# A decode kernel with attention over a long cache and a small MLP: each of the MLP's three tables read in two transfers instead of one

## The chip, the core and the metric

The kernel runs on one core of a Trainium2 chip. The metric is the device time of one execution in microseconds; the time shown for a kernel is the median of its runs. A profile is one further execution, recorded instruction by instruction and packet by packet. Its times count from the first instruction, and its span ends with the last one.

## The reference, cut to what matters

One token `x` of 448 numbers goes through two branches, which a gate mixes:

```
q = x @ wq                                   # 16 heads of 256
p = softmax(q . k_cache / 16)                # 8 K/V heads, 65536 cached positions each
a = (p @ v_cache) @ wo
h = layernorm(x)
u = gelu(h[d] * w1[f] + b1[f])               # 448 x 1792
b = sum over f of u[d, f] * w2[f]  + b2
g = sigmoid(sum(x * gate_w))
out = g * a + (1 - g) * b
```

The cache is 512 MB in bf16 (K and V, 8 heads, 65536 positions, 256 numbers). `wq` and `wo` are 3.5 MB each. The small MLP's `w1`, `b1` and `w2` are 1792 numbers each, 3.5 KB.

## The kernel before, in words

**The stream.** The cache is cut into 32 blocks of 16384 positions. A block of K, and a block of V, is 8 MB, 64 KB on each of 128 partitions. SBUF has one place for a block of V (`vt`) and three half places for K (`k_all`, slots 0 to 2). Blocks of K and V are fetched in turn by SyncE's queue (SP): `load_k_whole` (L132) and `load_v` (L135). For each block VectorE (DVE) transposes K (L402), TensorE (PE) forms the scores (L410), a softmax follows, and PE multiplies the probabilities into V (L430). Blocks 0 to 29 run in a loop of 15 turns with two blocks each (L597); the last two blocks are written out behind it.

**The start.** Before the loop stands work that is done once. SP issues three transfers: the tail of `wq` (`wq_t`, L159, 0.5 MB), the rest of it (`wq_m`, L162, 3 MB), and block 0 of K, called K0 here (L174, which calls L132). V0 is fetched inside the loop, at its first turn. ScalarE (ACT) issues the small transfers from its own queue: `x` (L158), the three tables (L168), the two halves of `gate_w` (L170) and `b2` (L173). Behind them on ACT stand a table load and a square root (L264) for the layer norm, then 14 GELU activations (L280) and the gate's exponential (L340).

**The tables.** Each table is brought in as 14 rows of 128 numbers, 256 bytes a row, and the three stand one below the other in `tables` (42 rows). One PE product with an identity (L255) turns them into columns, in `hd_ps`. DVE copies the columns out (L265, L266), goes on with the layer norm (L267 to L274, then L275, which writes `h_bc`), and ACT applies the GELU of `h_bc` with a column of `w1` as scale and one of `b1` as bias. `w2`'s columns are the weights of 14 PE products (L344).

**The order of work.** `seq` chains the instructions of each engine in the order in which the program is written. On PE the product of the tables (L255) stands ahead of the 128 products that form `q` (L291, L298), and these ahead of the MLP's products (L344). On DVE the copy L265 stands ahead of the rest of the layer norm, of the copies that place `q`, of the gate's sum (L338, L339) and of `mixer_tail` (L349 to L360), which the built program puts before the loop. At the loop's entry all engines meet at a barrier.

**The counters of the transfers.** The framework has eight completion counters for transfers and deals them out in turn. A transfer that is dealt a counter for a second time is not issued until the earlier transfer with that counter has landed; its queue waits there, with everything behind it. Before the loop they are dealt so:

| counter | 0 | 1 | 2 | 3 | 4 | 5 | 6 | 7 | 0 again | 1 again |
|---|---|---|---|---|---|---|---|---|---|---|
| transfer | x | wq_t | w1 | b1 | w2 | wq_m | gate_w a | gate_w b | b2 | K0 |

So `b2` (ACT) waits for `x`, and K0 (SP) for `wq_t`.

Of the kernel before, what the change touches and what calls it, by code (L numbers as in the profile page):

```python
# [33 lines left out]
def kernel(  # L34
# [15 lines left out]
    nc = tc.nc  # L50
# [5 lines left out]
    NF = F // 128  # L56
# [6 lines left out]
    def seq(ins):  # L63
        e = ins.ins.engine
        if e in last:
            tc.add_manual_dep(
                ins.ins,
                last[e],
                mybir.DependencyInfo(
                    mybir.DependencyClass.NoSync, mybir.DependencyReason.DATA  # L70
                ),
                reason="program order",
            )
        last[e] = ins.ins.name
        return ins
# [31 lines left out]
    tables = const.tile([3 * NF, 128], BF16)  # L107
# [43 lines left out]
    def load_v_last(n):  # L151
# [8 lines left out]
        out=wq_t[:, :], in_=A_wq[DM:D, :].rearrange("r (h n) -> (r h) n", h=2)  # L160
    ))
    seq(nc.sync.dma_start(out=wq_m, in_=A_wq[0:DM, :].rearrange("(p k) n -> p k n", k=3)))  # L162
    for k, table in enumerate((
        B_w1[0].rearrange("(b p) -> b p", p=128),
        B_b1.rearrange("(b p) -> b p", p=128),
        B_w2.rearrange("(b p) o -> b (p o)", p=128),
    )):
        seq(nc.scalar.dma_start(out=tables[k * NF:(k + 1) * NF, :], in_=table))  # L168
    for n0, n1 in ((0, D // 2), (D // 2, D)):
        seq(nc.scalar.dma_start(  # L170
            out=gw[:, n0:n1], in_=gate_w.rearrange("(o n) -> o n", o=1)[:, n0:n1]
# [14 lines left out]
        out=val[:], in_=rowsel[:, :, :, 0:NI], op=ALU.add, axis=AXIS.XY  # L186
    ))
    fst = const.tile([128, 2, REP], FP32)
    for e in range(2):
        seq(nc.vector.tensor_reduce(  # L190
            out=fst[:, e, :], in_=rowsel[:, :, :, e:e + 1], op=ALU.add, axis=AXIS.XY
# [3 lines left out]
        out=par[:], in_=ident_f[:].rearrange("p (a r) -> p r a", r=REP), op=ALU.add, axis=AXIS.X  # L195
# [3 lines left out]
        out=nval[:], in0=val[:], scalar1=-scale, scalar2=None, op0=ALU.mult  # L199
# [7 lines left out]
        out=same[:], in_=val[:].unsqueeze(1).to_broadcast([128, 64, REP])  # L207
# [8 lines left out]
        out=sel[:],  # L216
        in_=ident.rearrange("p (w k) -> p w k", w=NW).unsqueeze(2).to_broadcast([128, NW, NQ, 32]),
# [7 lines left out]
        out=xrr[:], in_=xr[:, DM:D].unsqueeze(2).to_broadcast([1, D - DM, 2])  # L225
    ))
    x_col = hd_ps[:, 40:44]
    for k in range(3):
# [13 lines left out]
        out=xtm[:], in0=par[:], scalar1=x_col[:, 3:4], scalar2=None, op0=ALU.mult  # L242
# [19 lines left out]
        out=veps[:], in0=mv[:, 1:2], scalar1=1e-5, scalar2=None, op0=ALU.add  # L262
# [5 lines left out]
    for _ in range(2):  # L268
# [3 lines left out]
            out=ntmp[:], in0=ntmp[:], scalar1=-0.5, scalar2=1.5, op0=ALU.mult, op1=ALU.add  # L272
# [3 lines left out]
        out=h_bc, in0=xf, scalar1=mv[:, 0:1], scalar2=rstd[:, 0:1],  # L276
        op0=ALU.subtract, op1=ALU.mult,
    ))
    for b in range(NF):
        seq(nc.scalar.activation(  # L280
            out=gel[b], in_=h_bc, func=ACT.Gelu_apprx_tanh,
# [33 lines left out]
    for k in range(2):  # L315
        seq(nc.vector.tensor_copy(
            out=qq[:, :, :, k, :], in_=qq_ps.rearrange("p (w g r) -> p w g r", g=HKV, r=REP)
# [314 lines left out]
    for n in (L - 1, L):  # L632
# [9 lines left out]
        else:  # L642
            load_v_last(L)
            for c in range(2):
                seq(nc.sync.dma_start(
                    out=wo_sb[:, 1, c],
                    in_=A_wo.rearrange("(h p c) n -> h p c n", p=128, c=2)[HQ - 1, :, c],
# [3 lines left out]
        else:  # L651
            def rest_base():
# [9 lines left out]
                out=lsv[:], in0=val[:], scalar1=lsum[:, 0:1], scalar2=None, op0=ALU.mult  # L662
# [8 lines left out]
                out=rdv[:], in0=rdv[:], scalar1=gcol[:, 0:1], scalar2=None, op0=ALU.mult  # L671
# [6 lines left out]
    for c in range(2):  # L678
# [9 lines left out]
        out=oT[:], in0=o_last, in1=rdv[:].unsqueeze(1).to_broadcast([128, 2, REP]), op=ALU.mult  # L688
# [43 lines left out]
```

## Time and profile before

| | |
|---|---|
| median of 3 runs | 1263.75 us (1263.6 to 1263.8) |
| span of the profiled execution | 1262.4 us |
| median less span | 1.35 us, which lie outside the first and the last instruction |
| PE busy | 820.4 us (65%) |
| DVE busy | 711.3 us (56%) |
| ACT busy | 75.7 us (6%) |
| read from HBM | 544.22 MB, 431 GB/s over the span |

Queue q1 holds SP's transfers and q10 holds ACT's. A transfer is split into packets on up to 16 rings, one on each DMA engine. On each ring a transfer ends with a packet of 4 bytes that counts it as landed there. The busy share of DMA is the mean over the 16 DMA engines; in a window of a few tenths of a microsecond it can pass 100%, because a packet is counted whole where it starts.

### The profile page before, as it was taken

Reading aid. Unit: us, or ns where it says so; the run is one execution under the profiler, and the core shown is the slowest. Engines: PE = TensorE matmul, PEld = TensorE weight load, DVE = VectorE, ACT = ScalarE, POOL = GpSimd, SP = SyncE. Lnnn points to the kernel's source line nnn. Section 1 sums busy time; section 2 is a strip of 40 time slices with the busy share of each in tenths; the row PEclk is TensorE's granted clock in tenths of the full one; section 3 lists DMA queues with packets and bytes.
Section 4 is the critical chain, followed back from the end, with each engine's and each line's share of the span. In section 5 each row is a group of like instructions: output and inputs, shape, how many; then the busy total and the mean of one; then the engine's idle time right before and its main releaser. Section 6 shows DMA issues by size and latency. Waiting matters only on the chain.

```text
span 1262.4 us, 12359 instructions
## 1 busy us (share of the span) xinstructions
PE 820.4 (65%) x4818; PEld 330.4 (26%) x4818; DVE 711.3 (56%) x755; ACT 75.7 (6%) x163; POOL 4.8 (0%) x9
## 2 busy tenths in 40 slices
PE   4756567575666746676565766648666576665668
PEld 2222122222222312222222322213222232221224
DVE  5665456654556644566544665446654456654575
ACT  4000000000000000000000000000000000000000
POOL 1000000000000000000000000000000000000000
PEclk9987787777887887888778787789777787877888
DMA  9999999999999999999999999999999999999998
GB/s 414 432 437 432 435 432 434 437 432 425 446 432 418 451 416 436 430 437 436 435 432 439 432 432 439 432 439 432 432 439 432 439 432 432 439 432 435 423 432 355
DMA packets 11768, 544.36 MB, mean 431 GB/s; under 512 B 1548, under 2 KB 2062, under 8 KB 2926
## 3 DMA queue, kind: packets, MB, share of 16 engines
q1 hardware_dynamic: 11666, 544.22, 99.7%
q8 instruction: 6, 0.10, 0.0%
q14 instruction: 4, 0.03, 0.0%
q10 hardware_dynamic: 92, 0.01, 0.0%
HBM read 544.22 MB, written 0.00 MB: 431 GB/s over the span
## 4 chain that ended last, share of the span: by engine, by line
DMA 69%; PE 13%; DVE 12%; issue 4%; SPq 0%; ACT 0%; DVEq 0%
DMA k_all<-in_A_k_cache_dram 67%; DVE kT L402 12%; PE sc L410 12%; DMA k_all<-in_A_v_cache_dram 2%; PE pv_last L555 0%; PE hd_ps L546 0%; PE f L555 0%; SPq L153 0%; PE f L693 0%; PE sm_ps L532 0%; ACT p_sb L498 0%; DVE rmax L467 0%; SPq L132 0%; PE hd_ps L532 0%; PE sm_ps L485 0%
## 5 line engine op out<-in xcount | busy, mean ns | idle before, releaser
L410 PE MATMUL sc<-kT,qz 128*128 128x512 bf16 x2048 | 545.7, 416 | 320.1 <-DVE kT L402 319.9
L402 DVE STREAM_TRANSPOSE kT<-k_all 128x2048 f32<-128x2048 f32 x256 | 570.9, 2283 | 208.3 <-DMA k_all<-in_A_k_cache_dram 159.0
L410 PEld LDWEIGHTS <-qz 128*128 128x128 bf16 x2048 | 211.2, 103 | 653.4 <-issue 474.2
L430 PE MATMUL pv_ps<-vt,pT 128*4 128x512 bf16 x1968 | 170.9, 523 | 27.2 <-DVE pT L505 27.2
L511 DVE SCALAR_TENSOR_TENSOR acc<-acc,al,pv_ps 128x512 f32<-128x512 f32 x31 | 23.2, 748 | 159.3 <-PE pv_ps L430 159.3
L430 PEld LDWEIGHTS <-pT 128*4 128x4 bf16 x2000 | 56.6, 108 | 128.9 <-issue 82.7
L498 ACT ACTIVATE p_sb<-sc,nb 128x512 bf16<-128x512 f32 x32 | 22.0, 687 | 1022.6 <-DVE nb L494 1022.6
L467 DVE TENSOR_REDUCE rmax<-sc 128x1 f32<-128x512 f32 x32 | 22.1, 692 | 63.7 <-PE sc L410 63.7
L505 DVE STREAM_TRANSPOSE pT<-p_sb 128x512 bf16<-128x512 bf16 x32 | 22.8, 711 | 27.1 <-ACT p_sb L498 27.1
L517 PE MATMUL hd_ps<-lsum,same 128*128 128x1 f32 x30 | 7.6, 322 | 28.8 <-DVE lsum L506 28.8
L485 PE MATMUL sm_ps<-mrun,ones_f 1*128 1x2 f32 x64 | 12.1, 256 | 21.2 <-DVE mrun L484 13.0
L471 PE MATMUL sm_ps<-ident_f,rmax 128*1 128x128 f32 x32 | 8.6, 270 | 24.5 <-DVE rmax L467 24.5
L555 PE MATMUL pv_last<-wo_in,steps 128*128 128x448 bf16 x64 | 15.6, 368 | 5.4 <-PEq L597 5.4
L555 PEld LDWEIGHTS <-steps 128*128 128x128 bf16 x128 | 11.6, 101 | 22.6 <-issue 14.4
L485 PEld LDWEIGHTS sm_ps<-mrun,ones_f 1*128 1x128 f32 x64 | 9.4, 182 | 27.4 <-DVE mrun L484 16.3
L550 DVE TENSOR_TENSOR a_acc<-a_acc,hd_ps 1x448 f32<-1x448 f32 x15 | 9.1, 608 | 12.9 <-PE hd_ps L546 12.9
L546 PE MATMUL hd_ps<-wo_sb,oT 128*1 128x448 bf16 x60 | 16.4, 365 | 0.0
L559 ACT CAST wo_sb<-pv_last 128x448 bf16<-128x448 f32 x16 | 8.5, 532 | 122.8 <-PE pv_last L555 122.8
L555 PE MATMUL f<-wo_in,steps 128*128 128x448 bf16 x64 | 15.5, 367 | 0.0
L562 ACT COPY wo_sb<-wo_sb 128x896 bf16<-128x896 bf16 x15 | 14.1, 937 | 15.3 <-PE hd_ps L546 15.3
L542 DVE CAST oT<-hd_ps 128x2 bf16<-128x2 f32 x15 | 2.4, 159 | 21.0 <-PE hd_ps L532 21.0
L517 PEld LDWEIGHTS hd_ps<-lsum,same 128*128 128x128 f32 x30 | 6.3, 261 | 30.1 <-DVE lsum L506 30.1
(124 smaller groups left out, 197.2 us busy)
## 6 DMA issues: line engine op xcount, KB each, us to landing
k_all<-in_A_k_cache_dram SPq DMA_DIRECT2D x2, 4096.0 KB, 16.1
vt<-in_A_v_cache_dram SPq DMA_DIRECT2D x1, 5120.0 KB
k_all<-in_A_v_cache_dram SPq DMA_DIRECT2D x1, 4096.0 KB
wo_in<-in_A_wo_dram SPq DMA_DIRECT2D x15, 224.0 KB, 27.9
vt<-in_A_wq_dram SPq DMA_DIRECT2D x1, 3072.0 KB, 10.5
vt<-in_A_v_cache_dram SPq DMA_DIRECT2D x1, 3072.0 KB
k_all<-in_A_v_cache_dram SPq DMA_DIRECT2D x1, 2048.0 KB
k_all<-in_A_v_cache_dram SPq DMA_DIRECT2D x1, 1024.0 KB, 22.6
```

Of the source, the lines that this page charges most:

```text
L402: seq(nc.vector.transpose(out=kT_tiles[i % 2][:].rearrange("p j w k c -> p (j w k c)").bitcast(FP32), in_=slots[pair[i // 4]][:, i % 4 * N ...
L410: seq(nc.tensor.matmul(sc_tiles[e][:, :], lhsT=qz[:, 2 * w + c, 2 * (NI - i):2 * (NI - i) + 128], rhs=kT_tiles[i % 2][:, :, w, :, c], star ...
L430: seq(nc.tensor.matmul(dst[32 * grp:32 * grp + 2 * REP, :, :], lhsT=pT[:, 32 * jj + 2 * REP * ip:32 * jj + 2 * REP * (ip + 1)], rhs=pairs( ...
L467: seq(nc.vector.tensor_reduce(out=rmax[:], in_=sc_ps[:, :], op=ALU.max, axis=AXIS.X))
L485: seq(nc.tensor.matmul(sm_ps[:, 128:128 + REP], lhsT=ones_f[0:1, :], rhs=mrun[0:1, :], start=True, stop=True))
L498: seq(nc.scalar.activation(out=p_sb[:, :], in_=sc_ps[:, :], func=ACT.Exp, scale=scale, bias=nb[:, 0:1], accum_out=den[:, 0:1],))
L505: seq(nc.vector.transpose(out=pT[:, :], in_=p_sb[:, :]))
L511: seq(nc.vector.scalar_tensor_tensor(out=acc[:], in0=acc[:], scalar=al_tiles[e][:, 0:1], in1=src[:, :, :], op0=ALU.mult, op1=ALU.add,))
L517: seq(nc.tensor.matmul(hd_ps[:, 460:461], lhsT=same[:].rearrange("p a r -> p (a r)"), rhs=lsum[:, 0:1], start=True, stop=True,))
L546: seq(nc.tensor.matmul(a_ps, lhsT=oT[:, c, r:r + 1], rhs=wo_sb[:, r, c, :], start=(r == 0 and c == 0), stop=(r == REP - 1 and c == 1),))
L555: seq(nc.tensor.matmul(wo_ps[c], lhsT=steps[:, WS - u:WS - u + 128], rhs=wo_in[:, 2 * u + c, :], start=(u == 0), stop=(u == WS - 1),))
L562: seq(nc.scalar.copy(out=wo_sb[:, 0], in_=wo_sb[:, 1]))
```

## The change

Each table is read in two transfers, cut at a row that differs from table to table: 12 and 2 rows of `w1`, 8 and 6 of `b1`, 4 and 10 of `w2`. The rows land where they did before. ACT issues six transfers where it issued three; the bytes and the rows are the same. Lines behind the edit move down by three.

```diff
-    for k, table in enumerate((
-        B_w1[0].rearrange("(b p) -> b p", p=128),
-        B_b1.rearrange("(b p) -> b p", p=128),
-        B_w2.rearrange("(b p) o -> b (p o)", p=128),
+    for k, (cut, table) in enumerate((
+        (12, B_w1[0].rearrange("(b p) -> b p", p=128)),
+        (8, B_b1.rearrange("(b p) -> b p", p=128)),
+        (4, B_w2.rearrange("(b p) o -> b (p o)", p=128)),
     )):
-        seq(nc.scalar.dma_start(out=tables[k * NF:(k + 1) * NF, :], in_=table))
+        for r0, r1 in ((0, cut), (cut, NF)):
+            seq(nc.scalar.dma_start(
+                out=tables[k * NF + r0:k * NF + r1, :], in_=table[r0:r1, :]
+            ))
```

With three more transfers the counters are dealt differently. `w1a` is the first piece of `w1`, and so on:

| counter | 0 | 1 | 2 | 3 | 4 | 5 | 6 | 7 | 0 | 1 | 2 | 3 | 4 |
|---|---|---|---|---|---|---|---|---|---|---|---|---|---|
| transfer | x | wq_t | w1a | w1b | b1a | wq_m | b1b | w2a | w2b | gate_w a | gate_w b | b2 | K0 |

So now `w2b` waits for `x`, `gate_w a` for `wq_t`, `gate_w b` for `w1a`, `b2` for `w1b`, and K0 on SP's queue waits for `b1a`. The product of the tables (L255 before, L258 after) waits for six transfers instead of three. The order of instructions on PE and DVE is the same.

## The prediction

> **What bounds the kernel now.** I read the page first (slices, chain of waits), then the windows, then the time order of the first 50 us, then the DMA packets in narrow windows.
>
> ```profile
> span 1262.4 us, 12359 instructions
> DMA  9999999999999999999999999999999999999998
> DMA 69%; PE 13%; DVE 12%; issue 4%; SPq 0%; ACT 0%; DVEq 0%
> 60.00:1190.00 1130.00, 731.49 (x4141) 290.89 (x4134) 630.79 (x640) 55.88 (x129) 0.00 (x0) 0.81 1.00 434
> ```
>
> The last row is a window: its last two figures are the DMA share, 1.00, and 434 GB/s. From 60 to 1190 us the 16 DMA engines never rest, while PE and DVE do. So the end is set by the stream of K and V. Whatever fits under it costs nothing. A pause of the stream is never made up, because there is no idle time behind it: it comes out at the end one for one. The change touches the first microseconds, so the question is whether the stream pauses there. The queue that feeds it, in order of time (SPq is SP's issuing):
>
> ```profile
> 0.73 0.42 SPq L159 DMA_DIRECT2D vt<-in_A_wq_dram  x1
> 4.17 0.33 SPq L132 DMA_DIRECT2D k_all<-in_A_k_cache_dram  x1
> 27.06 0.35 SPq L135 DMA_DIRECT2D vt<-in_A_v_cache_dram  x1
> 45.11 0.34 SPq L132 DMA_DIRECT2D k_all<-in_A_k_cache_dram  x1
> ```
>
> These issue `wq_t`, K0, V0 and K1. The stream has a transfer in hand at all times only if each is issued before the one ahead has drained.
>
> ```profile
> q10 hardware_dynamic: 2, 0.00, 1.1%
> ...
> q1 hardware_dynamic: 1, 0.00, 15.0%
> ...
> DMA packets 16, 0.07 MB, mean 177 GB/s; under 512 B 0, under 2 KB 0, under 8 KB 16
> ...
> DMA packets 34, 1.05 MB, mean 2017 GB/s; under 512 B 18, under 2 KB 18, under 8 KB 18
> ...
> DMA packets 31, 0.99 MB, mean 1652 GB/s; under 512 B 15, under 2 KB 15, under 8 KB 15
> ```
>
> These are DMA windows. From 1.5 to 1.78 us q1 has started nothing (only q10 is listed); to 1.80 it has started one packet. So the first packet comes 1.06 us after the issue at 0.73. From 1.78 to 2.15 sixteen start, so the last ring follows within 0.36. From 10.84 to 11.36 there are 18 packets under 512 B: the 16 counts of `wq_m` and two of `gate_w`. There `wq` is over and K0 begins. From 30.2 to 30.8 stand 15 counts: K0 ends, 30.45 in the middle. V0, issued at 27.06, is ready on the rings at 28.1 to 28.5. It has some 2.2 us in hand, and that is all the slack of the start.
>
> **What the tables' transfers cost today.** The q10 packets:
>
> ```profile
> q10 hardware_dynamic: 14, 0.00, 7.9%
> ...
> q10 hardware_dynamic: 84, 0.01, 1.4%
> ...
> DMA packets 29, 0.37 MB, mean 723 GB/s; under 512 B 14, under 2 KB 14, under 8 KB 14
> ...
> q10 hardware_dynamic: 1, 0.00, 2.2%
> q10 hardware_dynamic: 2, 0.00, 5.3%
> q10 hardware_dynamic: 1, 0.00, 1.9%
> q10 hardware_dynamic: 1, 0.00, 1.4%
> ```
>
> The first row is 4.42 to 4.62: one row of `w1` on each of 14 rings. The second is 4.42 to 9.53: 84 packets, which is 3 tables x 14 rings x 2 (a row and its count). The third is 9.02 to 9.53, the last 14 of them, `w2`'s counts. So each ring gives q10 one packet and then q1 one packet: six turns at 4.42, 5.34 and so on to 9.02, 0.92 us apart, the time of one 24 KB packet of `wq_m`. A transfer costs a ring two turns, 1.84 us, however small it is. The single rows are 9.95 to 10.02, 10.88 to 10.92, 13.32 to 13.35 and 18.16 to 18.20. They are `gate_w` and `b2`, one-row transfers: turns 7, 8 and 9, 10, and 12 of one ring. The packets of K0 are 64 KB, so there a turn takes 2.42 us ((18.17 - 13.33) / 2). That these one-row transfers stand behind three tables on one ring, although two of the 16 rings carry no row, tells that a small transfer begins at the same ring each time. Call it ring 0.
>
> **The change, part by part.** Issuing first:
>
> ```profile
> 1.30 0.34 ACTq L168 DMA_DIRECT2D tables<-in_B_w_dram  x1
> 3.50 1.28 ACT L264 ACT_TABLE_LOAD   x1 [3.50 <-issue]
> 10.26 0.20 ACT L264 ACTIVATE sdev<-veps 128x1 f32<-128x1 f32 x1 [5.47 <-DVE veps L261]
> ```
>
> Three more issues at about 0.4 us are 1.2 us of ACT's queue. The counters add waits: `gate_w b` for `w1a` (turn 2 of the rings, counted by about 6), `b2` for `w1b` (turn 4, about 7.6). With landing and issue the table load of 1.28 us then ends near 9.6 instead of 4.78, still ahead of the square root at 10.26: nothing. Without that cover it would be 4.8 us of ACT.
>
> K0 now waits for `b1a`. On ring 0 the order is w1a, w1b, b1a, b1b, w2a, w2b (12, 2, 8, 6, 4 and 10 rows all reach rings 0 and 1), so `b1a` counts on turn 6, at 9.02 to 9.53.
>
> ```profile
> 10.03 0.10 PEld L255 LDWEIGHTS <-tables 42*128 42x128 bf16 x1 [1.99 <-issue]
> 10.29 0.19 DVE L265 COPY wb<-hd_ps 128x28 f32<-128x28 f32 x1
> 11.72 0.16 PEld L291 LDWEIGHTS <-vt 128*128 128x128 bf16 x3 [1.60 <-DMA vt<-in_A_wq_dram]
> 12.23 0.51 DVE L275 TENSOR_SCALAR k_all<-k_all,mv,rstd 128x448 f32<-128x448 f32 x1
> 12.78 9.23 ACT L280 ACTIVATE k_all<-k_all,wb 128x448 bf16<-128x448 f32 x14 [1.02 <-DVE k_all L275]
> 19.15 0.61 DVE L338 TENSOR_TENSOR k_all<-k_all,gw 1x448 f32<-1x448 f32 x1
> 25.30 0.61 DVE L360 TENSOR_TENSOR rest<-y_sb,rest 1x448 f32<-1x448 f32 x1
> ```
>
> A consumer starts 0.36 (`wq_m`: 11.36 to 11.72) to 0.50 us (the tables: 9.53 to 10.03) after the last count. K0 is thus issued at 9.4 to 10.0 instead of 4.17, and its packets are ready at 10.45 to 11.4. The rings finish `wq` at 10.84 to 11.36. The gap is between nothing and 0.5 us; I take 0, since ring 0, where `gate_w` sits, runs early (turn 6 at 9.05). So the 5.2 us of later issue lie under `wq_m`.
>
> Now the tables' landing, the term that counts. On ring 0 the tables now take 12 turns where they took six, and these are the turns that `gate_w` and `b2` end today: 7 at 9.97, 8 and 9 together at 10.90 (one on each side of `wq_m`'s count), 10 at 13.33, 11 at 15.75, 12 at 18.17. So `w2b` counts where `b2` does today, at 18.17, and the product L255 starts 0.50 later, at 18.67: 8.64 us late.
>
> Behind L255 on PE wait the products for `q`, which could have begun at 11.72: they begin near 18.9. On DVE L265 waits, and behind it the rest of the layer norm, so `h_bc` ends at 21.4 instead of 12.74. The GELUs run 9.23 us and end at 30.65 instead of 22.01. The end of the MLP on DVE (25.30 + 0.61) moves to 34.55. The gate's sum at L338 needs `gate_w b`, now turn 16, four turns of 2.42 after 18.17: 27.85, and with 0.4 it starts near 28.3 and is done by 29.6, under the GELUs. `b2`, turn 18, counts as K0 ends, 30.5, and is read near 32.5. Both hide, with 1 to 2 us to spare.
>
> All engines meet before the loop, so V0 is issued at 27.06 + 8.64 = 35.70 and ready at 36.75 to 37.1, 36.95 in the middle. K0 has drained at 30.45. The rings stand empty for 6.5 us (8.64 less the 2.2 in hand). K1 comes 18.05 us behind V0's issue, as today, under V0's 19.4 us (K0's 11.05 to 30.45, as many bytes), so no second pause follows.
>
> Sum: 0 (issues) + 0 (K0) + 6.5 (V0) = 6.5. On the span, 1262.4 to 1268.9. The median stands 1.35 above the span, so 1263.75 + 6.5 = **1270.2 us**.
>
> **The rivals.** *The pieces do not pile up* (no change). If K0 reaches ring 0 a little after 10.92, the ring has nothing else and the six packets left drain at once, near 11.2. If pieces begin at rings of their own, none has more than six turns. Either way L255 starts by 11.6, under 11.72, `h_bc` is 1.5 us late and V0's 2.2 us cover it. Time 1263.75 to 1264.3, say 1264.0. For it: K0 is ready only 0.05 to 0.5 us before the ring is free. Against: the one-row transfers did pile up.
>
> *A fixed price per transfer.* If K0's packets don't enter the ring's turns that early, each of three more transfers costs the 1.84 us seen beside `wq_m`: 5.5. L255 starts 5.5 late, less 2.2 gives 3.3: 1267.05. The Trainium skill, DMA: Bandwidth & Descriptors, section Anatomy of one DMA, gives a fixed cost of about 2.0 us for a DMA whatever its size; three of them would be 6 us and 1267.55 by the same sum, an estimate from that page. The trace agrees with it at 1.84 beside 24 KB packets and not beside 64 KB ones, where two turns took 4.84.
>
> *One turn more.* If turn 9 on ring 0 or 1 misses its place ahead of K0's first packet, `w2b` counts at 20.6. That is 11.1 us late, less 2.2, so 8.9: 1272.65. A ring that runs 0.3 late or a gap before K0 goes the same way.
>
> Faster by over 0.2% needs 2.5 us out of a stream that nothing here shortens.
>
> **How the numbers follow.** Forecast 0.67 (1270.2, its own range 1269.5 to 1271.2), no pile 0.14, fixed price 0.09, one more turn 0.07; 0.03 stay for a gain that I can't name. The range goes from 1266.9, just under the fixed price, to 1272.7, just over one more turn: some 0.8. About 0.2% (2.5 us) is what a measurement of this kernel can tell from no change. Slower by more: 0.67 + 0.09 + 0.07 = 0.83; within: 0.14; faster: 0.03.
>
> **What would show it.** The load of the tables on PE near 18.7 instead of 10.03; q10 packets at 13.3, 15.75 and 18.2 that are the tables' and further ones to 30; K0's issue near 9.5; V0's near 35.7; a few slots of empty DMA between 30.5 and 37 and none later. If L255 stands near 11.5 and V0's issue at 28.6, the pile did not form. If V0 is late and the time is not, the rule that a pause is never made up is wrong.

## The result and the profile after

| | before | after |
|---|---|---|
| median of the runs, measured side by side | 1263.89 us (14 runs, 1263.6 to 1264.55) | 1266.2 us (14 runs, 1265.24 to 1267.07) |
| ratio of the times | | 1.0017 (95% interval 1.001 to 1.0024) |
| span of the profiled execution | 1262.4 us | 1265.2 us (this execution took 1267.01 us) |

The kernel is 2.3 us slower. The prediction said 6.5. The direction held; the size did not, and the time lies below the predicted range. The runs after also spread over 1.8 us, twice as far as before.

The page of the kernel after, its span, its DMA slices and its chain of waits:

```profile
span 1265.2 us, 12364 instructions
DMA  9999999999999999999999999999999999999997
DMA 68%; PE 13%; DVE 12%; issue 4%; SPq 0%; ACT 0%; DVEq 0%
```

The stream of K and V still sets the end, and no slice shows a pause at the start. Only the last slice fell, from 8 to 7. The next views show where the 2.8 us of the traced execution come from. First SP's queue after (start, duration, line):

```profile
8.57 0.33 SPq L132 DMA_DIRECT2D k_all<-in_A_k_cache_dram  x1
28.77 0.35 SPq L135 DMA_DIRECT2D vt<-in_A_v_cache_dram  x1
46.97 0.34 SPq L132 DMA_DIRECT2D k_all<-in_A_k_cache_dram  x1
```

K0 is issued 4.40 us later than before and V0 only 1.71 us later (28.77 against 27.06), where the prediction said 8.64. The path to V0, in order of time:

```profile
6.98 1.28 ACT L267 ACT_TABLE_LOAD   x1 [6.98 <-DMA tables<-in_B_w_dram]
10.26 0.20 ACT L267 ACTIVATE sdev<-veps 128x1 f32<-128x1 f32 x1 [1.99 <-DVE veps L264]
11.77 0.10 PEld L258 LDWEIGHTS <-tables 42*128 42x128 bf16 x1 [3.73 <-DMA tables<-in_B_w_dram]
12.02 0.19 DVE L268 COPY wb<-hd_ps 128x28 f32<-128x28 f32 x1 [1.80 <-PE hd_ps L258]
14.48 9.23 ACT L283 ACTIVATE k_all<-k_all,wb 128x448 bf16<-128x448 f32 x14 [2.72 <-DVE k_all L278]
26.99 0.61 DVE L363 TENSOR_TENSOR rest<-y_sb,rest 1x448 f32<-1x448 f32 x1
```

The product of the tables starts at 11.77 (before 10.03, 1.74 later), the GELUs at 14.48 (12.78, 1.70 later), the end of the MLP at 26.99 (25.30, 1.69 later). The chain moved as one piece. The table load is hidden ahead of the square root at 10.26.

The pile of tables did not form. The packets of ACT's queue in two DMA windows of the kernel after, 3.38 to 3.65 and 10.85 to 11.10 us:

```profile
q10 hardware_dynamic: 24, 0.00, 7.4%
...
q10 hardware_dynamic: 22, 0.00, 7.1%
```

In the first window all 12 rows of `w1a` and their 12 counts go through, between the end of `wq_t` and the start of `wq_m` (before, the first rows came at 4.42). What let them through there is not shown. So `w1a` costs no turns, `b1a` counts by 8.22, and K0 is issued at 8.57 instead of the predicted 9.4 to 10.0. The second window is where `wq_m` ends. There 22 packets go through, where the kernel before had two:

```profile
q10 hardware_dynamic: 2, 0.00, 0.8%
```

These 22 are all that was left: the tail of the tables, both halves of `gate_w`, and `b2`. The trace's packet records put the one-row transfers, which all go over ring 0, close behind one another: the two halves of `gate_w` at 11.02 and 11.05 and `b2` at 11.07, each with its count, up to 11.08. In the kernel before, a 64 KB packet of K0 went in between there, and held the ring for 2.42 us.

So K0 took no turns between the small packets, although it had been issued at 8.57. Four rings still had small packets when `wq_m` was counted on them. The packets can be put in order on each ring, since each starts within some ns of the end of the one ahead. On these four, K0 starts 6 ns after the last small packet, at 10.94, 10.99, 11.01 and 11.09; on the others it starts 6 ns after `wq_m`'s count, the first at 10.87. Had K0 only come late, it would have had to come just then on each of the four. That is unlikely, and a second trace of the kernel after shows the same on four rings (11.00 to 11.44). So a late arrival hardly explains it; what held K0 back on these rings is not shown.

So far this is the rival "the pieces do not pile up", nearly to the figure: it had the product by 11.6 and V0's issue at 28.6. But it had the time at 1264.0, because V0's 2.2 us in hand should have covered the delay. They did not. The window from 30 to 36 us, where K0 ends and V0 begins, before and then after (start and end, length, busy time of PE, PEld, DVE, ACT and POOL, PE's clock, DMA share, GB/s):

```profile
30.00:36.00 6.00, 3.41 (x13) 2.15 (x13) 2.87 (x4) 1.47 (x2) 0.00 (x0) 1.00 1.17 493
```

```profile
30.00:36.00 6.00, 5.01 (x18) 2.86 (x17) 1.27 (x4) 2.00 (x3) 0.00 (x0) 1.00 1.11 427
```

The rate at which V0 starts is 66 GB/s lower, 13%, although it was issued 1.41 us before the first ring finished K0 (28.77 to 30.18; before 27.06 to 30.21, 3.15 us). The packet records show what that is: the 16 first packets of V0, 64 KB each, took 2.89 us in the mean instead of 2.56 (2.42 is the usual time), and the last of them started at 32.43 instead of 31.64. The rings also stood empty between K0 and V0, for 0.34 us in the mean (before 0.03). V0's second packets took 2.65 (before 2.44), the later ones 2.42 to 2.44. Against before, these three make 0.85 us. In this trace the rings also drift apart. Two windows of the kernel after, 50.1 to 51.2 and 51.2 to 53.2 us:

```profile
DMA packets 25, 0.85 MB, mean 775 GB/s; under 512 B 12, under 2 KB 12, under 8 KB 12
...
DMA packets 19, 0.93 MB, mean 467 GB/s; under 512 B 4, under 2 KB 4, under 8 KB 4
```

and one of the kernel before, 49.55 to 51.0 us:

```profile
DMA packets 32, 1.05 MB, mean 723 GB/s; under 512 B 16, under 2 KB 16, under 8 KB 16
```

The packets under 512 B are V0's counts, one for each ring. Before, all 16 come by 50.95. After, 12 come by 51.2 and four stragglers only by 53.12. From there on no ring rests (the DMA share from 60 to 1190 us is 1.00 in both kernels), so a ring that is late stays late:

```profile
60.00:1190.00 1130.00, 734.93 (x4121) 291.79 (x4125) 631.91 (x642) 56.63 (x132) 0.00 (x0) 0.81 1.00 434
```

At the end, in the packet records, the rings count the last block between 1258.42 and 1260.87 (mean 1259.18), before between 1257.78 and 1258.62 (mean 1258.15). The mean ring is 1.03 late and the last one 2.25. The last one decides: in both kernels the cast below starts 1.25 us after it.

The rest is in the tail, where the output is cast and sent. After, then before:

```profile
1262.12 0.34 ACT L703 CAST res<-f 1x224 bf16<-1x224 f32 x1 [10.84 <-PE f L696]
1262.95 0.32 SPq L704 DMA_DIRECT2D out_dram<-res  x1
```

```profile
1259.88 0.34 ACT L700 CAST res<-f 1x224 bf16<-1x224 f32 x1 [9.56 <-PE f L693]
1260.30 0.32 SPq L701 DMA_DIRECT2D out_dram<-res  x1
```

The cast ends at 1262.46 and the output is issued 0.49 us later; before it was 0.08. That is 0.41 us more with nothing to do for the stream. From the issue to the end of the span it takes 2.28 us, before 2.08. Last ring 2.25 + issue of the output 0.41 + 0.20 behind it = 2.86 us; the spans differ by 2.85. The traced execution was one of the longer ones; the medians differ by 2.3.

### The profile page after: what moved, and what is told of

Its sections match the earlier page's. It is cut to its first block, busy times and chain, and to the rows that moved or that the text cites. A ratio compares the mean times of both kernels' runs of the same rounds, so it can differ in the third digit from the quotient of the medians.

```text
span 1265.2 us, 12364 instructions
## 1 busy us (share of the span) xinstructions
PE 825.4 (65%) x4818; PEld 331.4 (26%) x4818; DVE 711.5 (56%) x755; ACT 75.7 (6%) x163; POOL 4.8 (0%) x9
## 4 chain that ended last, share of the span: by engine, by line
DMA 68%; PE 13%; DVE 12%; issue 4%; SPq 0%; ACT 0%; DVEq 0%
DMA k_all<-in_A_k_cache_dram 66%; DVE kT L405 12%; PE sc L413 12%; DMA k_all<-in_A_v_cache_dram 2%; PE pv_last L558 0%; PE hd_ps L549 0%; PE f L558 0%; SPq L153 0%; PE f L696 0%; PE sm_ps L535 0%; ACT p_sb L501 0%; DVE rmax L470 0%; SPq L132 0%; PE hd_ps L535 0%; PE sm_ps L488 0%
## 5 line engine op out<-in xcount | busy, mean ns | idle before, releaser
L558 PEld LDWEIGHTS <-steps 128*128 128x128 bf16 x128 | 11.6, 100 | 22.5 <-issue 14.3
```

Source lines behind the costliest of these rows:

```text
L558: seq(nc.tensor.matmul(wo_ps[c], lhsT=steps[:, WS - u:WS - u + 128], rhs=wo_in[:, 2 * u + c, :], start=(u == 0), stop=(u == WS - 1),))
```

## The experiments

Two theories stood against each other. In one (theory A in the expectations), V0's late issue is the cause: a transfer must be issued well before the rings run dry, or its first packets come late and slow. In the other, the cause lies in the edit elsewhere (theory B names K0's later issue): in K0's later issue, in the counters that are dealt differently, or in the six pieces themselves. "Lead" below is the time from V0's issue to the end of K0 on the first ring. All figures on single packets and counts come from the trace's packet records and hold to 0.01 us.

### Delay V0 alone, in the kernel before

The last GELU is done three times more, on the same data. That makes ACT 2.0 us longer and leaves every transfer as it was.

```diff
-    for b in range(NF):
+    for b in list(range(NF)) + [NF - 1] * 3:
```

> The kernel before, with the last GELU done three times more (3 x 0.66 us on ACT), so that only the loop's entry and V0's issue move, from 27.06 to about 29.0; K0's issue and the tables stay. Theory A (the loss is V0's late issue: a large transfer's packets are ready ring by ring over some us after its issue, the rings drift apart and the last ring ends the stream): slower by 2 to 3.5 us, 1265.9 to 1267.4, and the counts of V0 spread over about 3 us instead of 1.3. Theory B (the loss is K0's late issue, 8.57 instead of 4.17, and the order in which the rings begin K0): no change, 1263.7 to 1264.3. The prediction's rule (2.2 us in hand, then one for one): no change, 1263.8.

Measured: 1265.94 us against 1264.06, ratio 1.0012 (1.0003 to 1.0021). V0 is issued at 29.44, a lead of 0.73 us. The window from 30 to 36 us:

```profile
30.00:36.00 6.00, 5.78 (x20) 3.16 (x19) 0.50 (x3) 1.94 (x3) 0.00 (x0) 0.50 1.03 406
```

V0's first packets took 2.96 us in the mean, and the last ring ended at 1260.39, 1.77 later than before. The output's issue follows the cast by 0.07 as before. So a late V0 alone, without any split table and with K0 at its old place, costs 1.9 us of median. The rate at the changeover falls as it does after the change (406 against 493).

The expected spread did not come: V0's counts lie 1.44 us apart, not about 3 (before 1.34). The rings end late together, 1.36 us in the mean. So a late V0 need not pull the rings apart to cost time.

### Give V0 its lead back, in both kernels

Three GELUs and three of the products that sum the MLP are left out.

```diff
-    for b in range(NF):
+    for b in range(NF - 3):
         seq(nc.scalar.activation(
...
-        for b in range(NF):
+        for b in range(NF - 3):
             seq(nc.tensor.matmul(
-                y_ps, lhsT=w2b[:, b:b + 1], rhs=gel[b], start=(b == 0), stop=(b == NF - 1)
+                y_ps, lhsT=w2b[:, b:b + 1], rhs=gel[b], start=(b == 0), stop=(b == NF - 3 - 1)
```

In the kernel after:

> The changed kernel with the last 3 of 14 GELUs and their 3 products left out (that part of the MLP is not computed), which brings V0's issue from 28.77 back to about 26.8 while the split tables and K0's issue at 8.57 stay. Theory A: back to the time before, 1263.5 to 1264.4. Theory B: the loss stays, 1265.5 to 1266.8.

In the kernel before:

> The kernel before with the same 3 GELUs and 3 products left out: the control of the run with 3 fewer, and the other side of V0's issue, about 25.1 instead of 27.06. Theory A: the lead of 3.2 us before K0 has drained was already nearly enough, so 0 to 0.6 us faster, 1263.2 to 1263.9. Theory B: no change, 1263.9.

Measured: after with three fewer 1265.03 us, ratio 1.0006 (0.9997 to 1.0015); before with three fewer 1263.93, ratio 1.0002 (0.9993 to 1.0011). The median of the first misses its expected range by 0.6 us. Its trace shows a stream as that of before: lead 3.39, first packets 2.48 us, last ring at 1258.41 (before 1258.62). What remains in the trace is the tail: the output is still issued 0.49 us behind the cast. So this run alone is half an answer: of the 2.3 us, 1.0 is left in the median, and the tail explains 0.4 of it. The traced execution, at 1264.6, was shorter than the median, and no trace shows the other 0.6. The second says that a lead beyond the 3.15 us of before gains nothing that can be measured. Two of its eleven runs, though, took 1266.39 and 1266.79 us, as long as the kernel after, with V0 issued early. Neither was traced, so something other than V0's lead may cost as much now and then.

### Let the pile form

The kernel after, with `gate_w` read in one transfer and `b2` set to 0 on chip instead of being read. With two transfers fewer the counters fall so that K0 waits for `w1a` and not for `b1a`.

```diff
-    for n0, n1 in ((0, D // 2), (D // 2, D)):
-        seq(nc.scalar.dma_start(
-            out=gw[:, n0:n1], in_=gate_w.rearrange("(o n) -> o n", o=1)[:, n0:n1]
-        ))
-    seq(nc.scalar.dma_start(out=b2b[:], in_=B_b2.rearrange("(o n) -> o n", o=1)))
+    seq(nc.scalar.dma_start(out=gw[:, :], in_=gate_w.rearrange("(o n) -> o n", o=1)))
+    seq(nc.gpsimd.memset(b2b[:], 0.0))
```

> The changed kernel with gate_w in one transfer and b2's transfer left out (b2 is taken as 0), so that the counters are dealt otherwise and K0 waits for w1a, issued near 4.2 instead of 8.57. The prediction's pile (with K0 ready in the queue, a ring gives q10 one packet between two 64 KB packets of K0): the tables' product on PE near 16 to 18.7, V0's issue at 33 to 35.7, 1268 to 1271. Theory A alone, if the rest of the tables still drains between wq_m and K0: product near 11.8, 1265.5 to 1266.8. Theory B: product near 11.8 and the time of before, 1263.9.

Measured: 1268.68 us, ratio 1.0033 (1.0021 to 1.0045). In order of time:

```profile
4.01 0.33 SPq L132 DMA_DIRECT2D k_all<-in_A_k_cache_dram  x1
16.04 0.10 PEld L255 LDWEIGHTS <-tables 42*128 42x128 bf16 x1 [7.96 <-DMA tables<-in_B_w_dram]
32.62 0.35 SPq L135 DMA_DIRECT2D vt<-in_A_v_cache_dram  x1
```

ACT's packets in its DMA windows, 10.85 to 11.10 and 13.15 to 15.70 us:

```profile
q10 hardware_dynamic: 4, 0.00, 1.4%
...
q10 hardware_dynamic: 6, 0.00, 0.2%
```

Here is the predicted pile. With K0 issued at 4.01 its 64 KB packets take their turns when `wq_m` ends. `wq_m` ends at 10.77 on its first ring here, a little earlier than in the kernel after. From then to 11.0 ten packets of ACT's queue go through (six of them ahead of the first window), not 22. What is left of the tables comes a turn of 2.4 us later each, and the last of it counts at 15.65. The product starts at 16.04 and not at the predicted 18.67, one turn of 2.42 earlier: `w1a` again went through ahead of `wq_m`, which saved its two turns, and the rest began one turn later than the tables of before (5.27 instead of 4.42 in the packet records). V0 is issued 2.54 us after the first ring has finished K0, and its first packets follow 0.99 us after that. That is a true pause, and the last ring ends at 1262.62, 4.0 later than before. The Trainium skill, DMA: Bandwidth & Descriptors, section Queues, rings and completion order, says that a DMA engine takes turns, packet by packet, between the queues that have work for it; this trace agrees (2.4 us between the small packets). In the kernel after, the small packets ran on, up to nine in a row on ring 0, although K0 had been issued some 2.3 us before; whether K0's queue had work for that ring by then, no run shows.

### The tail: do the counters make it?

Theory C in the expectations says that the counters make the longer tail. The kernel before, with three reads of one number into a spare tile behind K0, so that the later transfers are dealt the counters that they have after the change:

```diff
     load_k_whole(0, 0)
+    spare = const.tile([1, 3], BF16)
+    for i in range(3):
+        seq(nc.sync.dma_start(out=spare[:, i:i + 1], in_=B_b2.rearrange("(o n) -> o n", o=1)))
```

> The kernel before with three one-number reads of b2 into a spare place, issued by SP behind K0: tables, K0's issue (4.1) and V0's (27.06) stay, only the counters of all later transfers are dealt three further, as in the changed kernel. Theory C (the end of the changed program is 0.5 us longer because of the counters): the output's issue comes 0.49 us behind ACT's last copy instead of 0.08, 1264.4 to 1264.8. Rival (it hangs on something else in the build): 0.08 us and 1263.9 to 1264.2.

The kernel after, with five such reads, so that the later transfers get back the counters of before:

> The changed kernel with five such reads, which brings the counters of the last transfers back to those of the kernel before; split tables, K0 near 8.5 and V0 near 28.8 stay. Theory C: 0.08 us between ACT's last copy and the output's issue, 1265.4 to 1266.0. Rival: 0.49 us and 1266.2.

Measured: 1264.33 us, ratio 1.0 (0.9991 to 1.0009), for the first, and 1265.39, ratio 1.0011 (1.0002 to 1.002), for the second. The tail of the first:

```profile
1260.08 0.34 ACT L703 CAST res<-f 1x224 bf16<-1x224 f32 x1 [9.85 <-PE f L696]
1260.49 0.26 SPq L704 DMA_DIRECT2D out_dram<-res  x1
```

The counters of after, with 0.07 us between cast and issue: the counters alone do not make the 0.49. The second brought the tail back to 0.07, and its eleven runs reach from 1263.76 to 1266.74. The traced one was the shortest, and there V0's lead was 1.72 us:

```profile
30.00:36.00 6.00, 4.88 (x17) 2.85 (x16) 1.40 (x4) 2.00 (x3) 0.00 (x0) 1.00 1.17 504
```

504 GB/s, first packets 2.46 us, last ring at 1258.54. So with all six pieces and K0 issued late there are executions that lose nothing, and 0.31 us of lead lie between that one and the traced execution of the kernel after.

### K0 late alone, in the kernel before

K0's issue is moved behind a small write that DVE makes into its tile once the layer norm's sums are done.

```diff
-    load_k_whole(0, 0)
...
     seq(nc.vector.bn_aggr(out=mv[:], in_=stats[:]))
+    seq(nc.vector.memset(slots[0][:, 0, 0:2], 0.0))
+    load_k_whole(0, 0)
```

> The kernel before with K0 held back (a small DVE write into its place behind L260), issued near 10.3 instead of 4.17, later than the changed kernel does (8.57); tables whole. Theory A (a large transfer needs some us of lead, else its first packets are late and slow): the rings wait 0.2 to 0.6 us at 11, K0's first packets take 2.5 to 3.3 us instead of 2.42, and the time is 0.7 to 1.5 us longer, 1264.7 to 1265.5. The prediction's 1.06 us from issue to first packet alone: 0 to 0.5, 1264.0 to 1264.5.

Measured: 1265.25 us, ratio 1.0008 (0.9999 to 1.0017). The interval just takes in no change; but the shortest of the eleven runs, 1264.93, is longer than 32 of the 33 runs of before. K0's issue and the tail:

```profile
10.08 0.33 SPq L132 DMA_DIRECT2D k_all<-in_A_k_cache_dram  x1
...
1260.46 0.34 ACT L702 CAST res<-f 1x224 bf16<-1x224 f32 x1 [9.96 <-PE f L695]
1261.29 0.32 SPq L703 DMA_DIRECT2D out_dram<-res  x1
```

K0 was issued later than in the kernel after, 0.8 us before the rings finished `wq`, and it shows the same sign as a late V0: first packets at 11.08 to 12.17, most of them of 2.5 to 3.4 us, and a last ring that ends 0.58 later than before (1259.20). In the kernel after K0 had 2.3 us and its first packets took 2.42 in the mean. In the five other traces with K0 issued at 8.4 to 8.9 they took 2.48 to 2.59; in the two of these in which V0 had a long lead the stream still ended at 1258.41 and 1258.46, no later than before. The tail of 0.49 us stands here too, with the counters of before. So neither the split nor the counters of after are needed for it.

### Lead and tail given back together

The kernel after with three GELUs and products left out and the five spare reads.

> The changed kernel with the 3 GELUs and products left out (that part of the MLP is not computed) and with the five spare reads, so that V0's issue and the end's counters are both as before and only the split and K0's issue near 8.5 stay. Theories A and C together: 1263.6 to 1264.3. If K0's later issue or the split costs by itself: 1264.5 to 1265.0.

Measured: 1264.04 us, ratio 0.9998 (0.9989 to 1.0008). Lead 3.50, first packets 2.47 us, last ring 1258.46, tail 0.07. The six pieces with K0 issued late cost nothing by themselves that can be measured. With V0's lead and the short tail both given back, the loss is gone. How it divides between the two in an average execution is not shown: the tail is 0.4 us of it in both traces of the kernel after, and the run with three fewer and no spare reads stood 1.0 us above before, of which the tail explains less than half.

### How much lead is enough

The kernel after and the kernel after with five spare reads were traced once more, and the kernel before was given one and six GELUs more.

> The changed kernel once more, for its trace: its executions lie between 1265.2 and 1267.1. Theory A (V0's first packets, late and slow, set the loss): the execution's span follows the spread of V0's counts over the rings; a spread near 3 us goes with a span near 1265, one near 1.5 us with a span near 1263.

> The changed kernel with the five spare reads once more, for its trace: its executions lie between 1263.8 and 1266.7, and the traced one was the fastest, with V0's first packets at 2.42 us. Theory A: where the span is 1263.5 or more, V0's first packets take more than 2.5 us and its counts spread over 2.5 us or more.

> The kernel before with the last GELU done once more: V0's issue near 27.8, some 2.4 us ahead of the first ring's end of K0. Theory A: 0 to 0.8 us longer, 1264.1 to 1265.0. Rival (a step: no loss as long as V0's first packet can be there in time, 1.06 us after its issue): no change, 1264.1.

> The kernel before with the last GELU done six times more: V0's issue near 31.4, behind the end of K0 on most rings. Theory A: the rings wait until 1.0 us after the issue, about 2 us, and V0's first packets take about 3.1 us instead of 2.42: 2.5 to 3.6 us longer, 1266.6 to 1267.8.

Measured: 1266.69 and 1266.04 us in one run each (before 1264.11); with one GELU more 1264.13, ratio 1.0 (0.9991 to 1.0009); with six more 1267.6, ratio 1.0028 (1.0017 to 1.0038). The same window, 30 to 36 us, for the kernel after once more:

```profile
30.00:36.00 6.00, 5.35 (x19) 3.01 (x17) 0.93 (x4) 2.00 (x3) 0.00 (x0) 1.00 0.96 351
```

for the kernel after with five spare reads once more:

```profile
30.00:36.00 6.00, 5.17 (x18) 3.01 (x17) 1.11 (x4) 2.00 (x3) 0.00 (x0) 1.00 1.01 395
```

for one GELU more:

```profile
30.00:36.00 6.00, 3.30 (x16) 2.10 (x15) 2.98 (x4) 1.74 (x3) 0.00 (x0) 0.93 1.19 515
```

and for six more:

```profile
30.00:36.00 6.00, 4.18 (x17) 2.40 (x17) 0.93 (x3) 1.06 (x2) 0.00 (x0) 1.00 0.57 198
```

Two expectations failed here. V0's counts lie 2.45 us apart in the kernel after once more, and 2.08 in the one with five spare reads, where about 3 and at least 2.5 were expected. With three GELUs more it was 1.44. So the spread does not set the loss; that V0's first packets are late and slow holds in all of them.

Put in order of V0's lead, with the packet records beside them:

| kernel | V0's issue | K0's first ring ends | lead | V0's 16 first packets, mean | last ring of the stream | 30 to 36 us, GB/s |
|---|---|---|---|---|---|---|
| before, 3 fewer | 25.51 | 30.07 | 4.56 | 2.42 | 1258.24 | |
| before | 27.06 | 30.21 | 3.15 | 2.56 | 1258.62 | 493 |
| before, 1 more | 28.02 | 30.08 | 2.06 | 2.45 | 1258.61 | 515 |
| after, 5 reads | 28.63 | 30.35 | 1.72 | 2.46 | 1258.54 | 504 |
| after | 28.77 | 30.18 | 1.41 | 2.89 | 1260.87 | 427 |
| after, 5 reads, again | 28.92 | 30.22 | 1.30 | 2.78 | 1260.37 | 395 |
| after, again | 29.10 | 30.30 | 1.20 | 2.90 | 1260.43 | 351 |
| before, 3 more | 29.44 | 30.17 | 0.73 | 2.96 | 1260.39 | 406 |
| before, 6 more | 31.82 | 30.23 | -1.59 | 3.08 | 1262.36 | 198 |
| after, K0 early | 32.62 | 30.08 | -2.54 | 3.09 | 1262.62 | 176 |

There is a step. Down to a lead of 1.72 us the stream's end does not move. From 1.41 us on it is 1.8 to 2.3 us late, and it stays there to a lead of 0.73. With a lead below nothing all rings stand empty, and the loss grows with the pause: from 0.73 to -1.59 it is 1.97 us for 2.32 us of lead, 0.85 for each. The kernel before and the kernel after lie on one curve. The same kernel, after with five reads, was caught on both sides, with leads of 1.72 and 1.30. That one change of lead goes with the wide spread of the runs after is likely, but only these four traces show it. The border is drawn by single traces, and by the first ring's end: measured to the mean ring's end of K0, 2.10 us were enough there (1.72 in the table) and 1.66 to 1.76 us were not (1.20 to 1.41).

## Why the prediction was right or wrong

- **"Whatever fits under it costs nothing" and "A pause of the stream is never made up": right,** with an addition. The end moved by what the last ring had lost at 30 to 53 us, and 1100 us of full stream did not mend it. But it is not the mean ring that counts. In the trace after, the rings were 1.03 us late in the mean, and the last one 2.25.
- **Issues, table load, square root at no cost: right.** The load ended at 8.26, ahead of 10.26.
- **K0 at no cost: right, and for a reason close to failing.** It was issued at 8.57, not at 9.4 to 10.0. Moved to 10.08 in the kernel before, it made the stream 0.6 us late.
- **K0's packets take turns with the tables', so that turns 10 to 12 come 2.42 us apart, `w2b` counts at 18.17 and the product starts at 18.67: wrong. This step failed.** K0 took no turn while a ring still had small packets, and the last of the tables drained at once, by 11.02. The product was 1.74 us late and not 8.64. The run with K0 at 4.01 shows that the arithmetic of the turns holds when K0 is issued early enough (product at 16.04). That 1.06 us from issue to first packet is enough was taken from a single row, on empty rings. What happened is the rival's picture, in which the packets left drain at once. Its reason, that K0 reaches ring 0 "a little after 10.92", is not shown: K0 followed the small packets on each of four rings to 6 ns. It was issued at 8.57, and by the 0.97 to 2.01 us that V0 took to empty rings (six GELUs more) it would have been there by 10.6, by this estimate.
- **Twelve turns on ring 0: wrong by two.** `w1a` went through ahead of `wq_m`, by 3.65, and cost none, so `b1a` counted at 8.22 and not at 9.02 to 9.53.
- **The path from the tables to V0 moves as one: right.** 1.74 at the product, 1.71 at V0's issue.
- **V0 "has some 2.2 us in hand": wrong, the second step that failed,** and it hit the rival "no pile" as well as the forecast. It rests on the same 1.06 us: V0 would be ready on the rings 1.06 to 1.4 us after its issue, and the lead left over was counted as free. By the table above 1.41 us of lead are too few, 1.72 are enough. What was in hand is between 1.4 and 1.7 us (3.15 less 1.72 and less 1.41); the change took 1.7. That the time went the way that was forecast is luck: with the 1.71 us by which V0's issue moved, the prediction's own sum gives no loss.
- **The size.** Where the forecast had one pause of 6.5 us, there is a loss at the changeover of V0 of 2.25 in the trace and 0.41 at the output's issue. The first is shown: a late V0 alone makes such a loss in the kernel before, and a lead of 3.4 to 3.5 us removes it in the traces of the kernel after. The second is seen in five of the traces (after twice, after with three GELUs fewer, with K0 early and with K0 late) and absent in the rest, among them one with the counters of after. Its cause is open.

Open too is why the first packets of a transfer that is issued too late are slow (2.8 to 3.1 us for 64 KB) and not only late. Why the step lies between 1.41 and 1.72 us is argued only: with the rings empty, V0 reached the first ring 0.97 us after its issue and the last one after 2.01 (six GELUs more), so with a lead of 1.41 some rings run dry before V0 reaches them, and they did stand empty for 0.34 us in the mean.

The Trainium skill, DMA: Bandwidth & Descriptors, section Anatomy of one DMA, gives a transfer issued on GpSimd's path a fixed cost of about 2.0 us, and its Rules for kernel authors say to issue early so that this overlaps. The transfers here are issued by SP and ACT, for which the prediction used this figure too. The step between 1.41 and 1.72 us of lead lies between that and the 1.06 us that the prediction took from the first packet; that it is the same cost is not shown.

## What to carry to other kernels

In a kernel that is bound by a stream of large transfers, read the lead of each issue against the end of the transfer ahead, ring by ring, and do not count the time to the first packet as all that the lead must cover: here 1.7 us were enough and 1.4 were not, by one trace on each side. In these traces a delay that eats into that lead costs a step at once, not in proportion, and it reaches the end of the kernel, where the last ring counts and not the mean. When small transfers are added, count also which completion counters the later transfers are dealt: here three more small reads moved the issue of an 8 MB transfer by 4.4 us, and whether the small packets then waited behind large ones hung on that.

## What the runs showed of the hardware that was not expected

- V0, issued 1.41 us or less before the first ring ran dry, had first packets of 2.78 to 3.09 us in the mean for 64 KB, against 2.42 to 2.56 with a lead of 1.72 us or more. The rings drifted apart to 2.95 us at V0's end after the change, against 1.34 before; with three GELUs more they were as late and only 1.44 apart.
- The rings do not get a new transfer at one time. With the rings empty, V0's first packets started 0.97 to 2.01 us after its issue (six GELUs more); K0's, issued at 10.08 with `wq` just ending, 1.0 to 2.1 us after.
- Most of the drift was kept through 1200 us of full stream: the rings ended 2.45 us apart after and 0.84 before.
- Small packets one behind another on a ring passed with a row and its count every 20 ns (256 bytes) to 27 ns (448 bytes); between 64 KB packets of another queue each took a turn of 2.4 us.
- K0, issued at 8.4 to 8.9, let the small packets of ACT's queue go first on rings that still had some at 10.8 to 11.4; issued at 4.0 to 4.2, it took turns with them.
- The issue of the last output followed the cast that it waits for by either 0.07 to 0.08 or 0.49 to 0.50 us, the same in both traces of each of the two kernels that were traced twice.
